# Later pooled attention for one batch, sums of squares on other engines, and a one-pass summation in a fused attention and two-layer kernel

## The chip, the cores and the metric

The kernel runs on one core of a Trainium2 chip. The metric is the device time of one execution in microseconds (us). The kernel before took 986.81, 987.01 and 991.75 us in three runs; the median is 987.01 us.

## The reference

Three parts follow one another, and each one's output is the next one's input. All matrices come in with 64-bit floating point weights, while `q`, `k`, `v` and `x` have 32 bits.

```
q, k, v: (4, 8, 576, 64)
out_d  = softmax(mean4(q) @ mean4(k).T / 8) @ mean4(v)    # pooled over groups of 4 positions
local  = softmax(masked(q @ k.T / 8, |i - j| < 4)) @ v     # 7 neighbours
x  = repeat4(out_d) + local                                # (2304, 512)
h  = x @ w_in                                              # (2304, 2048)
x  = (max(h, 0) + alpha * min(h, 0)) @ w_out               # (2304, 512), "layer one"
xn = x / sqrt(mean(x * x) + 1e-6) * rms_g
x  = (silu(xn @ w_gate) * (xn @ w_val)) @ w_o2             # d_ff 1536, "layer two"
```

## The kernel before, in words

**Numbers.** A large product runs in three passes of 16-bit matmuls: both factors are split into a high and a low 16-bit part (`split`: ScalarE writes the high part, VectorE the rest). Each factor is first scaled by a power of two that comes from a sum of its squares: of `v` for the attention's output (`scale_x`, from the tile `vm`), and of each weight piece (`s1`, `s2`). A weight piece is loaded as 64-bit numbers in two halves, decoded to 32 bits in a slot `wc` (`Piece.load`, `Piece.decode`), summed (`Piece.square`), scaled (`scale_in`, `scale_out`, `scale2`) and split. Layer one has twelve pieces, layer two has twelve more.

**Where the squares are summed.** For `v`, ScalarE squares half a head pair at a time and adds up along the row (L771 for batch 0 in `Dense.norm`, L606 for the others in `vnorm`). L771 uses the tile `T` as a place for the unwanted squares, and `T` is later filled with the transposed `q` and `k` (L787). For a weight piece, `square` has TensorE multiply the upper 16 bits of twelve 128-column blocks by themselves (L1121, into `sqps`), and VectorE reads the diagonal (L1122).

**Order of the program.** Batch 0 has its pooled and local attention as dense matmuls (`Dense`, three column blocks c = 0, 1, 2 of 192 positions). Stages `h0`, `h1`, `h2` compute `h` for these blocks (tile `hps`, L1336), `o0` and `o1` the second product of layer one (tile `acc`, L1349); stage `c3` does both for the first block of batch 1. Then come `m2` (layer two: `gps` L1428, `oacc` L1457) and `m1` (layer one) in turn, each for 384 positions. A matmul stage hands a share of the list `feed[stage]` out between its steps: weight pieces (`prep_out`, `prep2_tasks`), pooled attention of batches 1 to 3 (`down_tasks`), and local attention of 192 positions (`local_tasks`, groups 4 to 11).

**Local attention.** A group makes six products of `q` with `k` windows (896 elements each; VectorE L480 and GpSimd in turn), sums each over 64 with L491, takes the softmax, and makes six products with `v` (L528). A product `prod` lies as 2 positions x 7 neighbours x 64. The sum over the 7 neighbours is three adds on VectorE in place (L541, 384, 256 and 128 elements).

**What sets the order on an engine.** `issue_order` takes every instruction with its buffer and data dependencies, gives it a cost by a formula, and runs a list scheduler 20 times; the best order is fixed for each engine. An engine works through its list in that order, so an instruction that waits holds up all behind it.

**Slots.** The buffers `u0` to `u12` hold first the pieces of `w_in`, later other tiles, and at last layer two's weights: piece number k of layer two is decoded into one slot and its split parts go into the slot that piece k - 1 was decoded into (`RING`).

## Time and profile before

| | us |
|---|---|
| median of three runs | 987.01 |
| the profiled execution, its own time | 985.53 |
| its span, first to last instruction | 983.8 |
| TensorE (PE) busy | 934.7 |
| VectorE (DVE) busy | 680.0 |
| ScalarE (ACT) busy | 469.5 |
| GpSimd (POOL) busy | 139.3 |
| granted TensorE clock, mean | 0.987 of 2.4 GHz |

The profiled execution took 1.7 us more than its span: that much lies around the first and the last instruction. PE's busy time counts a matmul until its result has landed, so matmuls overlap in it, and a busy PE isn't PE at its peak. In the page's forty slices PE is at 3, 7, 7, 8, 8 and 8 tenths in the first six, and then at 9 or more.

### The profile page before, as it was taken

The page shows a single profiled execution, that of the slowest core. Times are in us where ns is not written, and L with a number is a line of the kernel's source. Part 1 is how long each engine was busy: PE and PEld are TensorE (multiplying, and loading weights), DVE is VectorE, ACT ScalarE, POOL GpSimd, SP SyncE. Part 2 cuts the span into 40 slices and gives each one's busy share as a digit, 9 for nine tenths or more (in the row PEclk, how much of TensorE's full clock was granted, in tenths as well). Part 3 has the DMA queues.
Part 4 walks back from the last instruction along what each step waited for, and adds up shares of the span by engine and source line. Part 5 has one row for each costly group of instructions (what it writes and reads, how often), then busy time and mean ns, then how long its engine had stood idle before and what let it go on. Part 6 is the DMA issues. An engine that isn't in the chain of part 4 may idle for free.

```text
span 983.8 us, 16822 instructions
## 1 busy us (share of the span) xinstructions
PE 934.7 (95%) x6562; PEld 605.3 (62%) x6562; DVE 680.0 (69%) x1461; ACT 469.5 (48%) x1099; POOL 139.3 (14%) x120
## 2 busy tenths in 40 slices
PE   3778889999999999999999999999999999999998
PEld 2567677689865555556666665555556666555554
DVE  2689878989999979999676899972343352442333
ACT  4779999867554661233485242221232432321322
POOL 4511011211211022332001222210000000000000
PEclk9987999999999999999999999999999999999999
DMA  9847555566120331221221111110000000000000
GB/s 229 239 121 218 150 169 161 194 208 194 53 89 13 102 122 60 81 65 37 61 97 33 49 37 47 32 32 1 11 22 2 1 1 1 1 1 5 29 1 32
DMA packets 54205, 73.81 MB, mean 75 GB/s; under 512 B 22682, under 2 KB 35630, under 8 KB 54126
## 3 DMA queue, kind: packets, MB, share of 16 engines
q1 hardware_dynamic: 54126, 72.74, 24.9%
q8 instruction: 51, 0.84, 0.3%
q14 instruction: 28, 0.23, 0.1%
HBM read 68.01 MB, written 4.72 MB: 74 GB/s over the span
## 4 chain that ended last, share of the span: by engine, by line
PE 72%; ACT 11%; DVE 8%; DMA 6%; issue 2%; SPq 1%; ACTq 0%; DVEq 0%
PE gps L1428 25%; PE acc L1349 16%; PE hps L1336 13%; PE oacc L1457 12%; DMA out_dram<-ob 3%; DMA sdv<-in_v_dram 2%; ACT dls L896 2%; ACT wr L1103 1%; DVE prod L541 1%; DVE w L376 1%; ACT wr L1106 1%; ACT wi L375 1%; ACT g L1340 1%; PE lsps L876 1%; PE avps L684 1%
## 5 line engine op out<-in xcount | busy, mean ns | idle before, releaser
L1336 PE MATMUL hps<-xt,wi 128*128 128x192 f16 (+1 forms) x1536 | 339.1, 290 | 7.4 <-DVE g L376 5.7
L1428 PE MATMUL gps<-x,w 128*128 128x384 f16 x1728 | 342.2, 326 | 0.8 <-DVE th L1439 0.4
L1349 PE MATMUL acc<-ghl,wo 128*128 128x384 f16 (+1 forms) x960 | 256.1, 310 | 2.4 <-ACT ghl L375 1.8
L1428 PEld LDWEIGHTS <-w 128*128 128x128 f16 x1728 | 169.0, 98 | 113.5 <-issue 1.9
L1457 PE MATMUL oacc<-w,uhl 128*128 128x512 f16 x630 | 190.6, 379 | 1.6 <-ACT ob L1513 1.6
L1336 PEld LDWEIGHTS <-wi 128*128 128x128 f16 x1536 | 148.1, 100 | 58.5 <-issue 8.6
L1349 PEld LDWEIGHTS <-wo 128*128 128x128 f16 x1344 | 129.7, 99 | 65.1 <-issue 4.9
L1342 DVE SCALAR_TENSOR_TENSOR hps<-g,oma,hps 128x192 f32<-128x192 f32 (+1 forms) x128 | 65.8, 516 | 68.8 <-ACT g L1340 68.1
L1437 ACT ACTIVATE th<-gps,tsc 128x384 f32<-128x384 f32 x72 | 41.7, 579 | 131.0 <-PE gps L1428 130.6
L1457 PEld LDWEIGHTS <-uhl 128*128 128x128 f16 x630 | 61.6, 98 | 66.3 <-issue 2.4
L1439 DVE SCALAR_TENSOR_TENSOR th<-th,gps 128x384 f32<-128x384 f32 x72 | 39.7, 551 | 90.5 <-ACT th L1437 89.8
L1448 ACT ACTIVATE uhl<-gps 128x384 f16<-128x384 f32 x72 | 41.7, 579 | 108.3 <-DVE gps L1442 97.9
L1340 ACT ACTIVATE g<-hps 128x384 f32<-128x384 f32 x96 | 47.3, 493 | 95.3 <-PE hps L1336 95.1
L480 POOL TENSOR_TENSOR prod<-cq,ckv 128x896 f32<-128x896 f32 x24 | 55.5, 2313 | 218.6 <-DVE ls L491 68.4
L528 POOL TENSOR_TENSOR prod<-ls,ckv 128x896 f32<-128x896 f32 x24 | 45.2, 1884 | 151.0 <-DVE lo L541 58.9
L1449 DVE TENSOR_TENSOR uhl<-gps,uhl 128x384 f16<-128x384 f32 x72 | 45.3, 630 | 27.8 <-ACT uhl L1448 27.4
L375 ACT ACTIVATE ghl<-hps,sc 128x384 f16<-128x384 f32 x72 | 41.8, 580 | 44.9 <-DVE hps L1342 44.0
L376 DVE SCALAR_TENSOR_TENSOR ghl<-hps,sc,ghl 128x384 f16<-128x384 f32 x72 | 44.2, 613 | 22.8 <-ACT ghl L375 22.4
L1349 PE MATMUL acc<-g,wo 128*128 128x384 f16 (+1 forms) x384 | 59.1, 286 | 0.0
L541 DVE TENSOR_TENSOR prod<-prod 128x384 f32<-128x384 f32 (+1 forms) x96 | 50.1, 535 | 2.9 <-POOL prod L528 2.9
L1103 ACT ACTIVATE wr<-wr 128x768 f32<-128x768 f32 (+1 forms) x48 | 42.3, 882 | 20.4 <-DMA wr<-in_moe_w_in_dram 10.4
L491 DVE TENSOR_REDUCE ls<-prod 128x14 f32<-128x896 f32 x48 | 51.1, 1075 | 0.0
(233 smaller groups left out, 1172.5 us busy)
## 6 DMA issues: line engine op xcount, KB each, us to landing
wr<-in_moe_w_out_dram SPq DMA_DIRECT2D x18, 512.0 KB
wr<-in_moe_w_in_dram SPq DMA_DIRECT2D x10, 768.0 KB
wr<-in_moe_w_gate_dram SPq DMA_DIRECT2D x8, 768.0 KB
wr<-in_moe_w_val_dram SPq DMA_DIRECT2D x8, 768.0 KB
ckv<-in_k_dram SPq DMA_DIRECT2D x7, 768.0 KB
ckv<-in_v_dram SPq DMA_DIRECT2D x7, 768.0 KB
wr<-in_moe_w_out_dram SPq DMA_DIRECT2D x20, 256.0 KB
out_dram<-ob SPq DMA_DIRECT2D x13, 256.0 KB
```

The source lines that it names most:

```text
L375: nc.scalar.activation(out=hi, in_=src, func=AF.Copy, scale=s)
L376: nc.vector.scalar_tensor_tensor(out=lo, in0=src, scalar=s, in1=hi, op0=ALU.mult, op1=ALU.subtract)
L480: engs[i].tensor_tensor(out=pr, in0=view(st["q"][:, j, t:t + TP], [[D, TP], [0, ND], [1, D]]), in1=view(st["k"][:, j, t:t + TP], [[D, TP], ...
L491: nc.vector.tensor_reduce(out=st["s"][:, j, t:t + TP], in_=st.pop(("p", i)), axis=AX.X, op=ALU.add)
L541: add = lambda o, a, c: nc.vector.tensor_tensor(out=o, in0=a, in1=c, op=ALU.add)
L1103: nc.scalar.activation(out=hi.bitcast(F32), in_=hi.bitcast(F32), func=AF.Prelu, scale=2.0 ** -112, alpha=2.0 ** 32)
L1336: nc.tensor.matmul(ps[:, j], wi[:, f + j, a, kk * 128:(kk + 1) * 128], x[:, b_, kk, c0:c0 + n], start=(i == 0), stop=(i == 3 * KK - 1))
L1340: nc.scalar.activation(out=g, in_=ps, func=AF.Relu, scale=-1.0)
L1342: nc.vector.scalar_tensor_tensor(out=ps[:, j], in0=g[:, j], scalar=oma[:, f + j:f + j + 1], in1=ps[:, j], op0=ALU.mult, op1=ALU.add)
L1349: nc.tensor.matmul(acc[e], wo_f(f)[:, a, e * 128:(e + 1) * 128], hl[:, b_], start=(f == 0 and i == 0), stop=(f == NF - 1 and i == 2))
L1428: nc.tensor.matmul(ps, w2_t[i0 + f // 3].rearrange("p a (k c) -> p a k c", k=KK)[:, a, kk, (f % 3) * 128:(f % 3 + 1) * 128], xh[:, b_, kk] ...
L1457: nc.tensor.matmul(acc[tt], t[:, a, tt * 128:(tt + 1) * 128], w[:, b_, f % 3], start=(f in first and i == 0), stop=(f in last and i == 2))
```

## The change

Five things change.

1. The sums of squares of `v` for batches 0 and 1 go from ScalarE to TensorE and VectorE (`vsum`: eight matmuls of 128 columns for each of four head pairs, then one VectorE read of the diagonal).
2. The sums of squares of layer two's twelve pieces go from TensorE and VectorE to ScalarE: one pass over 1536 elements, with the unwanted squares written into the slot that will hold the piece's split parts (`w2_tile`).
3. Batch 1's pooled attention (`d1`) loads into the slots `u3`, `u4`, `u5` and not into a part of `wo`, and stands in `h1`'s list, where it stood before the first matmul stage.
4. The sum over the 7 neighbours is one VectorE reduction that reads every 64th element.
5. The lists of the later stages are dealt out otherwise (layer two's pieces begin in `o0`, one local group of `m2` 0 goes to `m2` 1, one of `m2` 1 to `m1` 2); the scheduler has 40 rounds; four small VectorE steps of `pow2` and `scale2` are merged.

```
-def issue_order(tc, nc, groups, rounds=20):
+def issue_order(tc, nc, groups, rounds=40):
...
+    def vsum(b, h, x):
+        if h == 0:
+            vm_t[b] = att.tile([128, HP], F32, tag="vm", name="vm")
+        ps = ps_t.tile([128, 128], F32, tag="at", name="vqps")
+        up = x.bitcast(BF)[:, 1::2]
+        for i in range(8):
+            nc.tensor.matmul(ps, up[:, i * 128:(i + 1) * 128], up[:, i * 128:(i + 1) * 128], start=(i == 0), stop=(i == 7))
+        nc.vector.scalar_tensor_tensor(out=ps, in0=ps, scalar=1.0, in1=ident, op0=ALU.mult, op1=ALU.mult,
+                                       accum_out=vm_t[b][:, h:h + 1])
...
         def vnorm():
+            if solo_v:
+                st["buf"] = prod_p.tile([SH, 4 * SD + 4 * D], F32, tag="prod", name="dd")
+                vsum(b, h, st["v"].rearrange("p a j r -> p (a j r)"))
+                return
...
-            for a in range(2):
-                nc.scalar.activation(out=self.st[h]["T"][0:SH, 0, W:W + 8 * D], in_=vt[:, a * 8 * D:(a + 1) * 8 * D], func=AF.Square,
-                                     accum_out=vm_t[b][0:SH, 2 * h + a:2 * h + a + 1])
+            vsum(self.b, h, self.st[h]["v"])
...
         def square(self, acc):
+            if self.w is not w_in and self.w is not w_out:
+                nc.scalar.activation(out=self.junk[:, 0:UW], in_=self.c[:, 0:UW], func=AF.Square, accum_out=acc)
+                return
...
-    def local(g, mul="GVGVGV", av=True, tags=(None, None, None), **kw):
+    def local(g, mul="GVGVGV", av=False, tags=(None, None, None), **kw):
...
-    d1 = down(1, 5, tags=tuple(wd[:, i * 1024:(i + 1) * 1024] for i in range(3)))
+    d1 = down(1, 5, tags=("u3", "u4", "u5"))
     run_all(d0)
     run_all(pi)
...
-    run_all(d1)
...
-        "h1": weave(c2, po[1]),
-        "h2": weave(c3, po[2] + pr2[0]),
-        "o0": pr2[1][:20],
-        "c3": pr2[1][20:]+pr2[2],
-        ("m2", 0): weave(pr2[3], local(4) + local(5)),
-        ("m2", 1): down(2) + local(6) + local(7),
-        ("m1", 2): local(8),
+        "h1": weave(c2, po[1]) + d1,
+        "h2": weave(po[2],c3),
+        "o0": pr2[0]+pr2[1],
+        "o1": [],
+        "c3": pr2[2],
+        ("m2", 0): weave(pr2[3],local(4)),
+        ("m2", 1): local(5)+down(2)+local(6),
+        ("m1", 2): local(7)+local(8),
```

With `av=False` the sum over the neighbours is the branch of `red_av` that stood there unused:

```
nc.vector.tensor_reduce(out=st["o"][:, t:t + TP, j], in_=pr.rearrange("p t n d -> p t d n"), axis=AX.X, op=ALU.add)
```

**How the order moves.** First ScalarE's list just ahead of the first step of `h0` (`g<-hps`, the first read of a finished `hps`). In these names `dd` with `dsum` and `dd<-dd` are batch 1's pooled softmax, `wi` the split of `w_in`, `wr` the decoding of a weight half. Before:

```order
L634 ACTIVATE qkT<-qkps 128x144
L375 ACTIVATE xt<-dxs,sc 128x192
L375 ACTIVATE wi<-wc,swi 128x512
L375 ACTIVATE xt<-dxs,sc 128x192
L375 ACTIVATE wi<-wc,swi 128x512
L896 ACTIVATE dls,dlsum<-lsps,dlm 96x102 x2
L653 ACTIVATE dd,dsum<-sps,dm 72x144 x4
L896 ACTIVATE dls,dlsum<-lsps,dlm 96x102 x4
L663 ACTIVATE dd<-dd,dsum 72x144 x4
L1340 ACTIVATE g<-hps 128x384
```

and in the change:

```order
L373 ACTIVATE wi<-wc,swi 128x512 x3
L1109 ACTIVATE wr<-wr 128x768
L373 ACTIVATE wi<-wc,swi 128x512
L1112 ACTIVATE wr<-wr,nhalf 128x768
L373 ACTIVATE wi<-wc,swi 128x512 x2
L1109 ACTIVATE wr<-wr 128x256
L1109 ACTIVATE wr<-wr 128x768
L1109 ACTIVATE wr<-wr 128x256
L1112 ACTIVATE wr<-wr,nhalf 128x768
L1356 ACTIVATE g<-hps 128x384
```

Batch 1's softmax steps have left this place, and the decoding of `w_out` has come in.

Second, layer two's squares. Before, on TensorE in stage `c3`, the blocks of a piece (`sqps<-wc`) stand between the matmuls of layer one:

```order
L1121 LDWEIGHTS wc
L1121 MATMUL sqps<-wc 128x128
L1336 LDWEIGHTS wi
L1336 MATMUL hps<-xt,wi 128x192
L1349 LDWEIGHTS wo
L1349 MATMUL acc_3053<-ghl,wo 128x192
L1336 LDWEIGHTS wi
L1336 MATMUL hps<-xt,wi 128x192
L1121 LDWEIGHTS wc
L1121 MATMUL sqps<-wc 128x128
```

In the change they are gone there, and ScalarE's list in the same stage has a square (`w_3487,s_114<-wc`) between the split of the piece ahead (`w_3353<-wc`) and its own (`w_3487<-wc`):

```order
L1356 ACTIVATE g<-hps 128x384
L1112 ACTIVATE wr<-wr,nhalf 128x768
L373 ACTIVATE w_3353<-wc,sw_117 128x1536
L373 ACTIVATE ghl<-hps,sc 128x2x192
L1356 ACTIVATE g<-hps 128x384
L1123 ACTIVATE w_3487,s_114<-wc 128x1536
L373 ACTIVATE ghl<-hps,sc 128x2x192
L1109 ACTIVATE wr<-wr 128x768
L373 ACTIVATE w_3487<-wc,sw_117 128x1536
```

So a square now stands in line with the steps `g` and `ghl` that the matmuls of `c3` need.

Third, VectorE's list in a layer-two stage, `m2` 2. `th`, `gps` and `uhl` are the steps that the matmuls wait for. Before, with the three adds:

```order
L1439 SCALAR_TENSOR_TENSOR th<-th,gps 128x384
L541 TENSOR_TENSOR prod<-prod 128x2x192
L1442 SCALAR_TENSOR_TENSOR gps<-th,kap,gps 128x384
L528 TENSOR_TENSOR prod<-ls,ckv 128x896
L1449 TENSOR_TENSOR uhl<-gps,uhl 128x384
L541 TENSOR_TENSOR prod<-prod 128x2x2x64
L541 TENSOR_TENSOR prod<-prod 128x2x192
L541 TENSOR_TENSOR lo<-prod 128x2x64
L541 TENSOR_TENSOR prod<-prod 128x2x2x64
L1310 TENSOR_TENSOR ra<-x_7086,rps 128x384
L541 TENSOR_TENSOR lo<-prod 128x2x64
```

and in the change, with the one reduction `lo<-prod`:

```order
L1455 SCALAR_TENSOR_TENSOR th<-th,gps 128x384
L526 TENSOR_TENSOR prod<-ls,ckv 128x896
L1458 SCALAR_TENSOR_TENSOR gps<-th,kap,gps 128x384
L544 TENSOR_REDUCE lo<-prod 128x2x64
L1465 TENSOR_TENSOR uhl<-gps,uhl 128x384
L1326 TENSOR_TENSOR ra<-x_6914,rps 128x384
L544 TENSOR_REDUCE lo<-prod 128x2x64
L1326 TENSOR_TENSOR ra<-x_6914,rps 128x384
L526 TENSOR_TENSOR prod<-ls,ckv 128x896
L544 TENSOR_REDUCE lo<-prod 128x2x64
```

Two short adds fewer stand between the steps that TensorE needs, and each sum is one instruction.

## Rows read from the trace of the kernel before

**Rows 1.** The page's busy time of each engine, share of the span, instructions.
```profile
PE 934.7 (95%) x6562; PEld 605.3 (62%) x6562; DVE 680.0 (69%) x1461; ACT 469.5 (48%) x1099; POOL 139.3 (14%) x120
```

**Rows 2.** Busy time in stretches: us, PE, PEld, DVE, ACT, POOL, PEclk, DMA, GB/s.
```profile
57.00:84.00 27.00, 20.43 (x195) 17.51 (x191) 25.25 (x75) 22.54 (x89) 2.13 (x2) 0.75 0.45 129
84.00:124.00 40.00, 33.54 (x330) 27.11 (x329) 34.93 (x79) 39.92 (x108) 2.40 (x6) 0.87 0.65 187
124.00:166.00 42.00, 39.18 (x467) 34.05 (x468) 32.50 (x94) 40.12 (x120) 5.51 (x6) 1.00 0.59 175
166.00:226.00 60.00, 59.58 (x542) 46.17 (x540) 54.50 (x109) 43.46 (x77) 15.22 (x8) 1.00 0.57 191
226.00:265.00 39.00, 38.95 (x475) 37.93 (x473) 37.22 (x87) 28.77 (x42) 6.49 (x3) 1.00 0.39 123
265.00:353.00 88.00, 86.82 (x603) 53.99 (x603) 82.77 (x207) 50.84 (x117) 8.25 (x4) 1.00 0.24 73
...
427.00:496.00 69.00, 67.13 (x419) 40.68 (x417) 59.82 (x114) 28.18 (x67) 12.99 (x6) 1.00 0.20 58
...
569.00:642.00 73.00, 73.00 (x425) 42.08 (x424) 68.17 (x141) 21.50 (x42) 19.50 (x12) 1.00 0.12 31
```

**Rows 3.** Groups by line and shape: the squares of weight pieces on PE.
```profile
L1121 PE MATMUL sqps<-wc 128*128 128x128 bf16 x212 | 34.7, 232 | 2.9 <-DVE sqps L1122 2.1 <-DVE wc L1108 0.4 <-ACT outd L853 0.3
```

**Rows 4.** PE's instructions in order of time, in stage c3: start, duration.
```profile
238.01 0.22 PE L1121 MATMUL sqps<-wc 128*128 128x128 bf16 x1
238.07 0.24 PE L1336 MATMUL hps<-xt,wi 128*128 128x192 f16 x1
238.15 0.22 PE L1121 MATMUL sqps<-wc 128*128 128x128 bf16 x1
238.21 0.24 PE L1349 MATMUL acc<-ghl,wo 128*128 128x192 f16 x1
```

**Rows 5.** ACT's instructions in order of time: squares of v, first transposes.
```profile
14.30 0.63 ACT L771 ACTIVATE T<-sdv 72x512 f32<-72x512 f32 x1 [0.33 <-DMA sdv<-in_v_dram]
...
15.06 0.63 ACT L771 ACTIVATE T<-sdv 72x512 f32<-72x512 f32 x1
...
15.81 1.20 ACT L787 ACTIVATE T<-tps 128x288 f32<-128x288 f32 x2
...
62.29 0.66 ACT L606 ACTIVATE dd<-wo 72x512 f32<-72x512 f32 x1
...
63.07 0.63 ACT L606 ACTIVATE dd<-wo 72x512 f32<-72x512 f32 x1
```

**Rows 6.** The chain of waits between 80 and 84 us: start, length, what.
```profile
80.22 1.43 ACT dd L653 x8
...
82.94 1.22 ACT dd L663 x4
```

**Rows 7.** Groups by line and shape: ACT's pass over a piece of layer two.
```profile
L375 ACT ACTIVATE w<-wc,sw 128x1536 f16<-128x1536 f32 x12 | 18.9, 1574 | 6.1 <-DVE sw L366 6.1
```

**Rows 8.** Groups by line and shape, DVE: reduction of neighbouring elements; the three adds.
```profile
L491 DVE TENSOR_REDUCE ls<-prod 128x14 f32<-128x896 f32 x48 | 51.1, 1075 | 0.0
...
L541 DVE TENSOR_TENSOR prod<-prod 128x384 f32<-128x384 f32 x48 | 27.4, 573 | 2.9 <-POOL prod L528 2.9
...
L541 DVE TENSOR_TENSOR lo<-prod 128x128 f32<-128x128 f32 x48 | 25.1, 524 | 0.1
...
L541 DVE TENSOR_TENSOR prod<-prod 128x256 f32<-128x256 f32 x48 | 23.7, 496 | 0.0
```

**Rows 9.** Groups by line and shape: spread writes (L787), L674 without; L575 spread reads.
```profile
L787 ACT ACTIVATE T<-tps 128x288 f32<-128x288 f32 x16 | 10.0, 707 | 2.2 <-PE tps L786 2.0
...
L674 ACT ACTIVATE aT<-atps 72x288 f32<-72x288 f32 x24 | 9.3, 413 | 3.7 <-PE atps L672 3.7
...
L575 DVE TENSOR_TENSOR xs<-xps,outd 128x192 f32<-128x192 f32 x16 | 7.8, 488 | 0.7 <-PE xps L562 0.7
...
L575 DVE TENSOR_TENSOR xs<-xps,outd 128x64 f32<-128x64 f32 x16 | 4.0, 252 | 2.8 <-PE xps L562 2.8
```

More of the change, by code (lines that the diff above doesn't have):

```diff
@@ L360, in pow2 @@
     def pow2(x, e, s, p, src=None):
-        if src is not None:
-            nc.vector.tensor_scalar(out=x, in0=src, scalar1=LEAST, scalar2=None, op0=ALU.max)
         xb, eb_, sb = (t.bitcast(I32) for t in (x, e, s))
-        nc.vector.tensor_scalar(out=xb, in0=xb, scalar1=1, scalar2=0x7F800000, op0=ALU.logical_shift_right,
+        nc.vector.tensor_scalar(out=xb, in0=xb if src is None else src.bitcast(I32), scalar1=1, scalar2=0x7F800000, op0=ALU.logical_shift_right,
                                 op1=ALU.bitwise_and)
@@ L764, in norm @@
         def norm(self, h):
-            b = self.b
-            if h == 0:
-                vm_t[b] = att.tile([128, 2 * HP], F32, tag="vm", name="vm")
-                nc.vector.memset(vm_t[b], 0.0)
-            vt = self.st[h]["v"]
-            for a in range(2):
-                nc.scalar.activation(out=self.st[h]["T"][0:SH, 0, W:W + 8 * D], in_=vt[:, a * 8 * D:(a + 1) * 8 * D], func=AF.Square,
-                                     accum_out=vm_t[b][0:SH, 2 * h + a:2 * h + a + 1])
+            vsum(self.b, h, self.st[h]["v"])
             if h == HP - 1:
-                scale_x(b)
+                scale_x(self.b)
         def tr(self, h):
@@ L1139, with prep @@
     p2 = [w2_piece(i) for i in range(12)]
-    def prep(p, acc):
+    def prep(p, acc, junk=None):
         def ld(h):
@@ L1148, in sq @@
         def sq():
+            if junk is not None:
+                p.junk = junk()
             p.square(acc)
@@ L1218, in f @@
             y = s2[:, i:i + 1]
-            nc.vector.tensor_scalar(out=y, in0=over_parts(y), scalar1=LEAST, scalar2=None, op0=ALU.max)
             e, sc_ = eb2[:, i:i + 1], sw2[:, i:i + 1]
-            pow2(y, e, sc_, P_W)
+            pow2(y, e, sc_, P_W, over_parts(y))
             if i < 4:
@@ L1233, in scale2_all, with w2_tile, f @@
         nc.vector.tensor_reduce(out=col(INV2), in_=inv2, axis=AX.X, op=ALU.max)
+        nc.vector.tensor_scalar(out=col(INV2), in0=col(INV2), scalar1=LEAST * LEAST, scalar2=None, op0=ALU.max)
         nc.vector.reciprocal(col(TS), col(INV2))
         nc.vector.tensor_scalar(out=kap, in0=inv2, scalar1=col(TS), scalar2=2.0 ** -P_U, op0=ALU.mult, op1=ALU.mult)
+    def w2_tile(i):
+        def f():
+            w2_t[i] = wts.tile([128, 2, UW], F16, tag=f"u{RING[W2_AT[i]]}", name="w2")
+            return w2_t[i][:, 0]
+        return f
     def split2(i):
@@ L1239, in f @@
             p = p2[i]
-            w = wts.tile([128, 2, UW], F16, tag=f"u{RING[W2_AT[i]]}", name="w2")
-            w2_t[i] = w
+            w = w2_t[i]
             split(w[:, 0], w[:, 1], p.c, sw2[:, i:i + 1])
@@ L1247, in prep2_tasks @@
         for i in W2_ORDER:
-            out.append(prep(p2[i], s2[:, i:i + 1]) + [scale2(i), split2(i)])
+            out.append(prep(p2[i], s2[:, i:i + 1], w2_tile(i)) + [scale2(i), split2(i)])
         out[-1].append(scale2_all)
```

1 line of the change is left out of this document (added).

## The prediction

> **What bounds the kernel now.** I read the page's busy line first: PE is busy for 934.7 of 983.8 us, the others for 680 us or less [rows 1]. An average over the run doesn't say where those 934.7 us lie, so I read the busy time in stretches next, cut at the first residual step of each stage [rows 2]. Two regimes are to be seen there. From 166 us on PE has no gaps worth naming (59.58 of 60, 38.95 of 39, 86.82 of 88, 67.13 of 69, 73.00 of 73), so an instruction taken from PE there is time won, and one added is time lost. Ahead of 166 us it is ScalarE: 39.92 of 40 us, then 40.12 of 42, while PE has gaps and VectorE is at 34.93 and 32.50. So the start is paid in ScalarE's work, up to the point where PE is full.
>
> The third thing to see is VectorE behind the full PE. It holds 82.77 of 88 us and 68.17 of 73 in the stretches that carry local attention, 94% and 93%. In those stages I take 94% as what it can hold while it still serves PE in time: the traced kernel shows nothing fuller in a long stretch. Last I read durations by line and shape, and the order of both kernels for what stands in line with what.
>
> **The squares of layer two leave PE: -8 us.** 144 matmuls go. Each holds its own 0.22 us in the records, but matmuls overlap: the next one starts 0.06 us behind a squares matmul and 0.08 us behind a 192-column one [rows 4], so a slot costs 0.060 us. The group shows 212 such matmuls with a mean of 232 ns [rows 3]; 212 by 232 ns is 49 us where its busy time says 34.7, which again says that the records overlap. One piece (12 matmuls) falls ahead of 166 us, where PE has gaps. The other 132 by 0.060 us give **-7.9 us** straight off the full PE. The 64 matmuls that come in for `v` stand ahead of 166 us and cost PE nothing as long as its gaps there (6.5 us of 40, 2.8 of 42 [rows 2]) hold 64 by 0.060 = 3.8 us.
>
> **The same squares on ScalarE: +2 us (0 to +17).** One pass over 1536 elements is not in the trace with a square; the nearest row is the split's high part of the same shape, 1.574 us [rows 7]. Twelve are 18.9 us of ScalarE. One falls ahead of 166 us; of the rest ten stand in 166 to 265 us and just behind it, where ScalarE is busy for 43.46 + 28.77 = 72.2 of 99 us [rows 2]; with 10 by 1.574 = 15.7 that is 88, 89%, still below the 95% that it held in 124 to 166. So most is covered. But a square stands in front of `g` and `ghl`, and PE waits for these; now and then one will come late by its 1.57 us. I take one to two of them. If that cover is gone (every one delays PE), it is 11 by 1.574 = 17 us.
>
> **The start: -8 us (0 to -14).** ScalarE loses 16 passes over `v`: eight of L771 and eight of L606, each 0.63 to 0.66 us, at a spacing of 0.76 and 0.78 us [rows 5]. By durations that is 10.2 us, by spacings 12.3; I take 11. ScalarE gains, in the same stretch, one layer-two square (1.6) and, by the order, five splits of `w_out` that come forward (512 elements, 0.63 each by the L771 row, 3.2). Net -6.2. The first evacuation of transposes (L787 at 15.81) stood behind L771's writes to the same tile (14.30 to 15.69) [rows 5]; about 1.5 us of that go too, together **-8 us** until PE is full. At the most I add the pooled softmax `dd` that leaves the chain at 80 to 84 us, 1.43 + 1.22 = 2.65 us [rows 6], and the 3.2 us of splits if they were idle filling: -14. `d1` isn't gone, though: its loads, softmax and products come later in `h1`, where ScalarE was as full (40.12 of 42), so I count its move at nothing. Its place behind `h0` also takes its DMAs from `wo`'s space to `u3` to `u5`; DMA engines are busy 0.59 to 0.65 of that time [rows 2]. At the least it's 0: VectorE gets the diagonal reads and `d1`'s steps there, some 5 us by the order, on 34.93 of 40 and 32.50 of 42, and could come last instead.
>
> **The strided sum: +13 us (0 to +24).** This is the largest term, and the trace doesn't show its price. Three adds, 573 + 524 + 496 ns = 1.593 us, become one reduction over 896 elements that hops by 64 elements at each step [rows 8]. Below, the bound is the reduction of the same 896 elements in their order: 1.075 us [rows 8]. Above, there are two rows for spread access [rows 9]. A VectorE step that reads spread elements takes 488 ns for 192 elements and 252 for 64: (488 - 252) / 128 = 1.84 ns an element and 134 ns fixed, so 896 x 1.84 + 134 = 1.78 us. ScalarE's spread write of 288 elements takes 707 where the plain one takes 413, (707 - 413) / 288 = 1.02 ns an element more; laid on the reduction it is 1.075 + 0.914 = 1.99 us. I take 1.78: it is the same engine, and a read. By that the edit makes each sum longer, by 0.19 us, not shorter.
>
> The page titled "Vector Engine (DVE) Microarchitecture Reference" of the Trainium skill (section 5.2, measured stream behaviour on trn2) says the same more sharply: a port keeps its rate only for runs of two or more adjacent words, and one that hops at every element takes 1.73 to 1.76 ns, in one case 2.50. An estimate by these is 1.63 to 2.3 us for this reduction; the trace's 1.84 ns an element lies between.
>
> What it does in a stage depends on the deal of local groups too. `m1` 2 has two groups' worth, 12 reductions where 9 sums stood. Its VectorE is 59.82 of 69 us; less 9 x 1.593 = 14.3, plus 12 x 1.78 = 21.4, plus five more L491 (5.4) and some 3 us of other steps of the group that comes in: 75 of 69 us. `m2` 2 by the order has 12 where 8 stood: 68.17 - 12.7 + 21.4 = 77 of 73 us. The excess over the whole stretch is 6 + 4 = 10 us, over 94% of it 10.5 + 8.3 = 19; neighbours can take some over, so **+13**. At 1.075 both are 67 to 69 us, and the term is about 0; at 1.99 the excess is 10 + 8 to 15 + 13 us, and I take 24.
>
> The merged scale steps, the 40 rounds and the rest of the new deal I cost at nothing: they lie on VectorE ahead of the splits, which are early in stages where PE is fed by pieces long since there.
>
> **Sum.** -8 - 8 + 2 + 13 = -1 us against the profiled execution of 985.5, thus 984.5. The median of the runs lies 1.5 us above that execution, so against it the forecast is **986 us**. A measurement of this kernel can tell 0.5% from no change, so "same" is 982.1 to 991.9 us.
>
> **The rivals.**
>
> - **The stride costs nothing** (a reduction takes 1.075 us whatever it reads). For it: the kernel's other reduction runs at 1.2 ns an element. Against: the spread rows [rows 9]. Then the last term is 0: 985.5 - 8 - 8 + 2 = 971.5, against the median **973**, faster.
> - **VectorE becomes the bound, slower than before.** If a reduction takes 1.99 us, the price of the second spread row, or more, `m1` 2 and `m2` 2 are over-full by the 24 us above: 985.5 - 14 + 24 = 995.5, against the median **997**. For it: the row [rows 9], and VectorE at 94% in these stages. Against: PE's other stages have slack on VectorE that could take groups over (59.82 of 69). The point from which it decides is where 24 reductions' growth outweighs 14 us, near 1.8 us each. The same page's 2.50 ns would put it well beyond: an estimate by that is 2.3 us each.
> - **The squares hold ScalarE's queue.** A square writes into the slot that the piece before was decoded into, so it waits until VectorE has split that piece; `g` and `ghl` of the matmul stage wait behind it. If each of 11 costs its 1.574 us on PE, the term is 17 and not 2: 984.5 + 15 = 999.5, against the median **1001**. Against: 89% of ScalarE, and PE in `c3` has the work of two products.
> - **The start gives nothing** (VectorE or the DMAs come last there): 984.5 + 8, against the median **994**.
>
> **How the numbers follow.** The forecast gets 0.35; its own range, with the start from 0 to -14 and the sum from 1.7 to 1.85 us, is 978 to 994. The stride that costs nothing gets 0.33, VectorE as the bound 0.20, the queue of squares 0.06, the empty start 0.06. The cases lie on both sides, so the range must hold most: from 967 (the first rival with a start of -14) to 1003 (the second with a start of -2). Faster by over 0.5%: all of the first rival but a little, and a quarter of the forecast's, 0.40. Within 0.5%: over half of the forecast's and some of the empty start, 0.25. Slower: the second and third rivals, half of the empty start and a fifth of the forecast's, 0.35.
>
> **What would show it.** The squares: no `sqps` from `gps`' weights, and PE in 166 to 265 us with fewer instructions and no new gaps. The start: PE full some 8 us earlier than 166 us, with ScalarE as busy as before up to there. The strided sum: the mean of `lo<-prod` as a reduction, about 1.78 us; 1.08 makes the first rival right, 2 or more the second. `m1` 2 and `m2` 2: VectorE at 97% or more and PE with gaps that end on `th` or `uhl`. ScalarE's squares: gaps of PE that end on `g` or `ghl` between 166 and 300 us, 1.6 us each, if the queue is the trouble. The forecast is wrong if the reduction is far from 1.78 us, or if it is near it and PE in those two stages has no gaps.

## The result and the profile after

The changed kernel takes **998.24 us** (median of 4 runs, 995.70 to 1000.68) against 986.91 us for the kernel before: a ratio of 1.0109, 95% interval 1.0072 to 1.0146. It is slower, by 1.1%. The forecast was 986 us, with -1 us for the change. The forecast's range (967 to 1003) holds the time, but the change went the other way, and two of its terms were wrong in their mechanism. The profiled execution took 1000.68 us with a span of 998.8.

The page's busy line of the changed kernel:

```profile
PE 939.8 (94%) x6482; PEld 604.1 (60%) x6482; DVE 690.6 (69%) x1337; ACT 475.3 (48%) x1091; POOL 132.1 (13%) x120
```

VectorE is busy 10.6 us more than before [rows 1], ScalarE 5.8 more. PE has 80 matmuls fewer (144 less 64). The stretches of the changed kernel, cut at the same stage steps (us, PE, PEld, DVE, ACT, POOL, PEclk, DMA, GB/s):

```profile
125.00:171.00 46.00, 43.24 (x478) 35.92 (x475) 37.94 (x106) 43.90 (x148) 5.06 (x6) 0.96 0.47 136
171.00:229.00 58.00, 57.75 (x515) 44.60 (x514) 52.98 (x77) 45.68 (x78) 14.40 (x8) 1.00 0.62 201
229.00:270.00 41.00, 36.91 (x418) 34.88 (x416) 36.77 (x76) 34.81 (x50) 0.00 (x0) 1.00 0.42 137
270.00:345.00 75.00, 75.00 (x459) 44.80 (x457) 68.03 (x132) 36.66 (x59) 11.99 (x6) 1.00 0.09 32
...
427.00:502.00 75.00, 70.09 (x432) 42.41 (x430) 73.23 (x113) 24.93 (x53) 20.81 (x11) 1.00 0.19 57
...
578.00:655.00 77.00, 73.17 (x419) 41.44 (x418) 75.13 (x127) 20.11 (x40) 23.11 (x14) 1.00 0.15 39
```

Against [rows 2] two places stand out. The start is over at 171 and not 166 us. And PE has gaps in the stages that it filled before: 36.91 of 41, 70.09 of 75 and 73.17 of 77 us, in the last two with VectorE at 73.23 and 75.13, 98%. The groups by line and shape of the changed kernel that answer to [rows 3, 7, 8]:

```profile
L544 DVE TENSOR_REDUCE lo<-prod 128x128 f32<-128x896 f32 x48 | 82.8, 1727 | 0.0
...
L489 DVE TENSOR_REDUCE ls<-prod 128x14 f32<-128x896 f32 x48 | 51.2, 1077 | 0.0
...
L1123 ACT ACTIVATE w<-wc 128x1536 f16<-128x1536 f32 x12 | 17.8, 1485 | 7.0 <-DVE w L374 3.9 <-DVE ry L1309 2.5 <-DVE ry L1306 0.6
...
L1130 PE MATMUL sqps<-wc 128*128 128x128 bf16 x68 | 10.1, 271 | 4.8 <-DVE wc L1118 3.6 <-DVE sqps L1131 1.1
```

The strided reduction takes 1.727 us, the contiguous one 1.077; the square on ScalarE 1.485; of the 212 squares of `wc` on TensorE 68 are left, those of layer one. Who PE waits for between 427 and 655 us (engine, line, releaser: us, times, longest us):

```profile
PE xps L560 <- DVE lo L544: 2.8, 3, 1.3
PE hps L1352 <- DVE ghl L374: 2.5, 4, 0.9
PE gps L1444 <- DVE th L1455: 2.4, 2, 1.4
PE acc L1365 <- ACT ghl L373: 1.2, 1, 1.2
PE xps L560 <- DVE inv L1377: 1.1, 1, 1.1
```

7.7 of these 10.0 us end on VectorE's `lo`, `ghl` and `th`: the strided sums themselves and the steps that stand behind them.

To tell early from late I count from each profiled trace how much of PE's main work (the columns of `hps`, `acc`, `gps`, `oacc`, at 0.163 us per 384 columns, 798.0 us in all) has been started by 225 us, and call "lost late" what the rest of the span has beyond the rest of that work: (span - 225) - (798.0 - done). What is lost late thus holds PE's small matmuls and transposes too; the least in any kernel here is 44.1 us. A number in these two columns is worked out, not printed by a view, and comes from one execution, which can lie some us from the median (e4's took 1007.44 us, e7's 989.24); small differences in them are weak. "Time" is the median of the runs, the ratio that to runs of the kernel before on the same chip; it is not the quotient of the medians.

```
kernel                                    time    ratio (95%)               span   done 225  lost late
before                                   986.91                             983.8     90.3     51.1
changed                                  998.24  1.0109 (1.0072 - 1.0146)   998.8     87.7     63.5
e1  changed, adds                        981.17  0.9925 (0.9899 - 0.9952)   979.7     90.5     47.2
e2  changed, d1 at its old place         992.31  1.0056 (1.0036 - 1.0076)   990.7     92.2     59.9
e3  before, strided                     1008.15  1.0202 (1.0174 - 1.0231)  1001.7     93.9     72.6
e4  changed, w2 squares on PE           1001.59  1.0149 (1.0118 - 1.0180)  1005.4     88.1     70.5
e5  e1, v squares on ACT                 982.25  0.9962 (0.9941 - 0.9984)   980.2     90.0     47.2
e6  e1, d1 at its old place              981.38  0.9943 (0.9922 - 0.9963)   980.7     87.9     45.6
e7  e1, w2 squares on PE                 984.21  1.0001 (0.9975 - 1.0027)   987.5     89.2     53.7
e8  neighbours innermost                 982.21  0.9951 (0.9929 - 0.9972)   979.4     91.4     47.8
e9  e8 on GpSimd's, adds on the others   989.12  1.0033 (1.0009 - 1.0058)   992.2     82.8     52.0
e10 e1, diagonal reads five times        987.44  1.0015 (0.9988 - 1.0042)   986.8     80.3     44.1
e11 e1, old deal                         986.08  1.0011 (0.9986 - 1.0035)   983.7     92.0     52.7
e12 half the sums strided                998.39  1.0124 (1.0086 - 1.0163)   997.4     86.5     60.9
e13 changed, right price                 985.15  0.9985 (0.9969 - 1.0001)   983.8     88.8     49.6
e14 e1, extra ScalarE                   1000.20  1.0148 (1.0120 - 1.0175)  1002.8     71.1     50.9
e15 e1, extra VectorE                    985.89  0.9993 (0.9975 - 1.0011)   984.3     85.3     46.6
e16 e8, right price                      976.39  0.9906 (0.9879 - 0.9934)   974.9     92.4     44.3
e17 e12, right price                     992.45  1.0074 (1.0048 - 1.0100)   990.3     86.0     53.3
e18 e1, 3 rounds                         981.77  0.9964 (0.9939 - 0.9988)   981.4     86.9     45.3
```

So the change lost 2.6 us by 225 us and 12.4 after it, 15.0 in the spans.

### The profile page after: what moved, and what is told of

It is laid out like the page before. It is cut to its first block, busy times and chain, and to the rows that moved or that the text cites. A ratio compares the mean times of both kernels' runs of the same rounds, so it can differ in the third digit from the quotient of the medians.

```text
span 998.8 us, 16517 instructions
## 1 busy us (share of the span) xinstructions
PE 939.8 (94%) x6482; PEld 604.1 (60%) x6482; DVE 690.6 (69%) x1337; ACT 475.3 (48%) x1091; POOL 132.1 (13%) x120
## 4 chain that ended last, share of the span: by engine, by line
PE 58%; DVE 19%; ACT 10%; DMA 8%; issue 4%; SPq 1%; ACTq 0%; DVEq 0%
PE gps L1444 21%; PE hps L1352 12%; PE acc L1365 10%; PE oacc L1473 10%; DVE lo L544 7%; DMA out_dram<-ob 2%; DVE prod L526 2%; ACT wr L1112 1%; DMA sdv<-in_v_dram 1%; ACT dls L902 1%; ACT wr L1109 1%; DVE hps L1358 1%; DMA wr<-in_moe_w_gate_dram 1%; DVE gps L1458 1%; DVE wc L1114 1%
## 5 line engine op out<-in xcount | busy, mean ns | idle before, releaser
L1365 PE MATMUL acc<-ghl,wo 128*128 128x384 f16 (+1 forms) x960 | 247.8, 310 | 1.6 <-ACT ghl L373 1.2
L1444 PEld LDWEIGHTS <-w 128*128 128x128 f16 x1728 | 169.7, 99 | 122.3 <-issue 10.2
L1473 PE MATMUL oacc<-w,uhl 128*128 128x512 f16 x630 | 193.2, 379 | 2.5 <-ACT ob L1529 1.5
L544 DVE TENSOR_REDUCE lo<-prod 128x128 f32<-128x896 f32 x48 | 82.8, 1727 | 0.0
L478 POOL TENSOR_TENSOR prod<-cq,ckv 128x896 f32<-128x896 f32 x24 | 51.8, 2156 | 234.5 <-PE avps L697 54.2
L526 POOL TENSOR_TENSOR prod<-ls,ckv 128x896 f32<-128x896 f32 x24 | 41.5, 1727 | 145.8 <-DVE lo L544 66.6
```

The source lines that it names most:

```text
L478: engs[i].tensor_tensor(out=pr, in0=view(st["q"][:, j, t:t + TP], [[D, TP], [0, ND], [1, D]]), in1=view(st["k"][:, j, t:t + TP], [[D, TP], ...
L526: engs[i].tensor_tensor(out=pr, in0=view(st["s"][:, j, t:t + TP], [[ND, TP], [1, ND], [0, D]]), in1=view(st["v"][:, j, t:t + TP], [[D, TP] ...
L544: nc.vector.tensor_reduce(out=st["o"][:, t:t + TP, j], in_=pr.rearrange("p t n d -> p t d n"), axis=AX.X, op=ALU.add)
L1365: nc.tensor.matmul(acc[e], wo_f(f)[:, a, e * 128:(e + 1) * 128], hl[:, b_], start=(f == 0 and i == 0), stop=(f == NF - 1 and i == 2))
L1444: nc.tensor.matmul(ps, w2_t[i0 + f // 3].rearrange("p a (k c) -> p a k c", k=KK)[:, a, kk, (f % 3) * 128:(f % 3 + 1) * 128], xh[:, b_, kk] ...
L1473: nc.tensor.matmul(acc[tt], t[:, a, tt * 128:(tt + 1) * 128], w[:, b_, f % 3], start=(f in first and i == 0), stop=(f in last and i == 2))
```

## Experiments: the strided sum

**e1, the adds back.**

```
-    def local(g, mul="GVGVGV", av=False, ...
+    def local(g, mul="GVGVGV", av=True, ...
```

> The changed kernel with the three adds back; all else as changed. Theory S (the strided reduction, 1.727 us against some 1.39 to 1.59 for the adds, fills VectorE in the stages from the second layer-two stage to the fourth and costs the 15 us that the changed kernel's stage marks lose between 427 and 724 us): 998.2 - 15 = 983 us, 980 to 987, with VectorE at 95% or less in these stages. Rival D (the new deal of the local groups, two in one stage, costs it, whatever the sum is made of): 993 to 998 us, the loss still between 427 and 724 us.

981.17 us, ratio 0.9925: better than both kernels. Late loss falls from 63.5 to 47.2. The strided sum costs 16.3 us late, and the rest of the change is worth some 4 to 7 us (4.1 by the spans, 7.4 by the ratio). Rival D falls.

**e3, the stride alone.** The kernel before with `av=False`.

> The kernel before with the strided reduction in place of the three adds, nothing else. Theory S: each of 48 sums grows by 0.13 (1.727 - 1.593) to 0.34 us; where VectorE was at 93 to 94% the growth shows: 987 + 5 to 12, 992 to 999 us. Rival D (only the new deal overfills VectorE): 986 to 989 us, since the old deal had at most 8 to 9 sums a stage.

1008.15 us: more than either theory gave. The late loss grows by 21.5 us with the old deal's 8 or 9 sums in a stage. VectorE's time doesn't explain all of it: 48 sums of 1.719 us in place of 1.593 are 6 us, and the whole busy time rose by 697.9 - 680.0 = 17.9. How much of it is order (see e13) is not shown: this kernel was not run with another order.

**e8, no strided read.** The product is written so that the reduction reads neighbouring elements.

```
-            pr = prod_p.tile([128, TP, ND, D], ...)
+            pr = prod_p.tile([128, TP, D, ND], ...)
...
-                out=pr,
+                out=pr.rearrange("p t d n -> p t n d"),
...
-  tensor_reduce(..., in_=pr.rearrange("p t n d -> p t d n"), ...)
+  tensor_reduce(..., in_=pr, ...)
```

> The changed kernel, but each product of p and v is written with the 7 neighbours innermost, so that the reduction reads neighbouring elements and the product writes every 7th. If the stride is what costs 0.65 us a reduction: the reduction takes 1.08 us, as L489's does. The price may go to the product: 1.08 us to 1.7 on VectorE; GpSimd's half is off the path. Then 24 VectorE products cost 0 to 15 us, 48 reductions give 31: 998.2 - 17 or more, 970 to 985 us. If a reduction with 128 results costs 1.7 us whatever it reads: reduction 1.7 us, 998 us or more.

982.21 us, inside the expectation. Its groups (L526 is the product, L544 the sum):

```profile
L544 DVE TENSOR_REDUCE lo<-prod 128x128 f32<-128x896 f32 x48 | 51.4, 1073 | 0.0
...
L526 POOL TENSOR_TENSOR prod<-ls,ckv 128x896 f32<-128x896 f32 x24 | 44.9, 1873 | 135.8 <-DVE lo L544 60.0 <-DVE ls L520 38.4 <-issue 31.7
L526 DVE TENSOR_TENSOR prod<-ls,ckv 128x896 f32<-128x896 f32 x24 | 43.7, 1822 | 0.0
```

The reduction falls from 1.727 to 1.073 us, and VectorE's product, which now writes every 7th element, goes from 1.119 to 1.822. So the stride has its price on whichever side it is, read or write; on GpSimd the spread write takes 1.873, where the plain product took 1.884 in the kernel before and 1.727 in the changed one. VectorE does 673.8 us in all.

**e12, half of the sums strided** (those whose product GpSimd makes).

```
-            if av_pool:
+            if i % 2:
```

> The changed kernel with 24 of the 48 sums strided (those whose product GpSimd does not make, or the other half, in turn) and 24 by adds. If each strided sum costs TensorE its 0.35 us, whatever else VectorE does: half the loss, 989 to 991 us. If there is a limit of VectorE below which the stride is free: 24 x 0.25 = 6 us of VectorE are within its room, and the time is 981 to 984 us.

998.39 us: as much as with all. Both expectations missed, so the loss is neither proportional to the number of strided sums nor a plain limit on VectorE's time. Its groups show a second cost:

```profile
L544 DVE TENSOR_REDUCE lo<-prod 128x128 f32<-128x896 f32 x24 | 41.1, 1714 | 0.0
...
L526 DVE TENSOR_TENSOR prod<-ls,ckv 128x896 f32<-128x896 f32 x24 | 39.5, 1644 | 0.0
```

VectorE's products L526 take 1.644 us on the mean instead of 1.119. By the starts and ends of the records, the eleven that began while a GpSimd product was running took 1.41 to 2.72 us, the other 13 took 1.07 to 1.09 (more in the last section). None of the 24 strided reductions ran beside a GpSimd product here.

**e9, each way where it is cheaper.** The layout of e8 for GpSimd's products, plain products and adds for VectorE's (`if engs[i] is not nc.gpsimd`).

> The changed kernel with each of the two ways where it is cheaper: products made on GpSimd are written with the neighbours innermost (GpSimd took 1.87 us for that, 1.73 for the plain ones) and reduced in 1.07 us; products made on VectorE stay plain and are summed by the three adds. VectorE does 24 x 0.5 = 12 us less than with the adds alone. If VectorE still holds TensorE up with the adds: 972 to 978 us. If with the adds the later stages are TensorE's and VectorE's time there is worth nothing: 980 to 982 us, as with the adds alone.

989.12 us: both missed. VectorE's busy time is 691.2 us where the reckoning made it 668: the 15 of its products that met one of GpSimd's took 1.94 us on the mean. And 7.7 us are gone by 225 us, nearly all of it ahead of the local attention that the edit changes. Another order of one and the same program moved that by 3.6 us (e18 below); the rest is not explained.

**e13, the planner told.** This came of e3 and e12. `issue_order` prices a VectorE instruction by

```
            return 89 + n / (1.92 if fast else 0.96) + 60 * (extra > 0)
```

with n its elements: 89 + 896 / 0.96 = 1022 ns for a sum, strided or not, and 489 + 356 + 222 = 1067 for the three adds. Whoever reads that expects a small gain. The edit:

```
+            if n == 896 and any(list(a.ap)[-1][0] > 1 for a in (o, ins[0])):
+                return 89 + 1.83 * n
             return 89 + n / (1.92 if fast else 0.96) + 60 * (extra > 0)
```

> The changed kernel, strided sums as changed, but the planner's formula prices such a reduction at 1.73 us and not at 1.02. If the order made for a wrong price is what costs (steps that TensorE needs put behind sums that end 0.7 us later than planned): most of the 17 us comes back, 983 to 988 us. If it is VectorE's time: 995 to 1000 us as before.

**985.15 us**, 13 us less than the changed kernel, with the same instructions: 48 strided sums of 1.723 us. Of the 16.3 us of late loss 13.9 go (63.5 to 49.6). VectorE's time is not what came back: it is busy for 700.1 us here, 9.5 more than in the changed kernel. The difference is in the order. From 427 to 655 us PE's waits add up to 4.5 us, where the changed kernel has 10.0 and the kernel before 3.0. VectorE's instructions in order of time in the same stage, first the changed kernel (start, duration, no idle time between):

```profile
443.36 1.08 DVE L526 TENSOR_TENSOR prod<-ls,ckv 128x896 f32<-128x896 f32 x1
444.37 1.71 DVE L544 TENSOR_REDUCE lo<-prod 128x128 f32<-128x896 f32 x1
445.99 0.62 DVE L374 SCALAR_TENSOR_TENSOR ghl<-hps,sc,ghl 128x384 f16<-128x384 f32 x1
446.51 1.76 DVE L544 TENSOR_REDUCE lo<-prod 128x128 f32<-128x896 f32 x1
448.16 0.64 DVE L1358 SCALAR_TENSOR_TENSOR hps<-g,oma,hps 128x384 f32<-128x384 f32 x1
448.68 1.11 DVE L526 TENSOR_TENSOR prod<-ls,ckv 128x896 f32<-128x896 f32 x1
449.69 1.72 DVE L544 TENSOR_REDUCE lo<-prod 128x128 f32<-128x896 f32 x1
451.30 0.64 DVE L374 SCALAR_TENSOR_TENSOR ghl<-hps,sc,ghl 128x384 f16<-128x384 f32 x1
```

Then with the right price:

```profile
443.53 0.61 DVE L1360 SCALAR_TENSOR_TENSOR hps<-g,oma,hps 128x384 f32<-128x384 f32 x1
444.05 1.74 DVE L546 TENSOR_REDUCE lo<-prod 128x128 f32<-128x896 f32 x1
445.71 0.60 DVE L376 SCALAR_TENSOR_TENSOR ghl<-hps,sc,ghl 128x384 f16<-128x384 f32 x1
446.23 1.07 DVE L528 TENSOR_TENSOR prod<-ls,ckv 128x896 f32<-128x896 f32 x1
447.23 0.61 DVE L1360 SCALAR_TENSOR_TENSOR hps<-g,oma,hps 128x384 f32<-128x384 f32 x1
447.76 1.71 DVE L546 TENSOR_REDUCE lo<-prod 128x128 f32<-128x896 f32 x1
449.38 0.60 DVE L376 SCALAR_TENSOR_TENSOR ghl<-hps,sc,ghl 128x384 f16<-128x384 f32 x1
```

In the changed kernel a product and a sum stand in a row, with no step that PE needs (`hps` or `ghl`) between them. By the formula the two take 2 x 1.02 = 2.04 us, on the chip 1.73 + 1.08 = 2.8. In the lines with the right price such a step stands on either side of each sum: `hps` and `ghl` get their turn every 1.5 to 2.2 us (443.53, 445.71, 447.23, 449.38) and not every 2.2 to 3.1 (445.99, 448.16, 451.30). In the four densest batches of six sums of the changed kernel the first and the last start 12.4 to 12.9 us apart, in the same four batches of e13 13.3 to 17.7. What that does to PE, busy time of 443 to 459 us by engine, in the changed kernel:

```profile
443.00:459.00 16.00, 14.29 (x88) 8.59 (x87) 16.00 (x17) 3.68 (x7) 5.62 (x4) 1.00 0.14 46
```

and in e13:

```profile
443.00:459.00 16.00, 16.00 (x102) 9.93 (x100) 16.00 (x20) 4.29 (x8) 5.86 (x3) 1.00 0.16 50
```

VectorE is full in both; PE runs 88 matmuls in the one and 102 in the other. A full VectorE costs PE little as long as what PE needs comes first.

Could it be one lucky order? The late column speaks against it: the five kernels with strided reads at the old price (changed, e2, e3, e4, e12) lose 59.9 to 72.6 us late, and every other kernel, in whatever order, 44.1 to 53.7. e17 and e16, the other two with the new price, come next.

**e17, half strided, told.** e12 with e13's edit.

> The kernel with 24 strided sums and 24 by adds, and the planner told 1.73 us for a strided one. If the wrong price was what cost in the untold one (998.4 us): 983 to 987 us, between the adds alone (981) and all strided with the right price (985). If VectorE's 24 slower products beside GpSimd are what cost there: 994 us or more.

992.45 us: 6 us of the 17 come back, neither expectation's number. The order was part of it. What is left (late loss 53.3, done by 225 us 86.0) is not told apart here from the slower two-source steps beside GpSimd (VectorE's products still took 1.40 us on the mean) and the order's luck.

**e16, neighbours innermost, told.** e8 with e13's edit.

> The kernel whose products are written with the neighbours innermost, the planner told 1.73 us for a VectorE product that writes every 7th element (it was priced at 1.02 and took 1.82; 24 of them). If a wrong price costs where VectorE is short: below the 982.2 us of the untold one, 976 to 980 us. If the room that the cheap reduction (1.07 us) leaves has hidden the wrong price: 980 to 983 us.

**976.39 us**, ratio 0.9906 (0.9879 to 0.9934): the best of all, faster than the kernel before by 0.9% and than the changed one by 2.2%. Against e8 the price alone gave 5.8 us. The page's busy line of it shows VectorE 3 us below the kernel before and PE at 929.9:

```profile
PE 929.9 (95%) x6482; PEld 598.9 (61%) x6482; DVE 677.0 (69%) x1337; ACT 475.7 (49%) x1091; POOL 136.1 (14%) x120
```

## Experiments: squares, deal and start

**e4 and e7, layer two's squares back on TensorE** (`square` without its early return), in the changed kernel and in e1.

> The changed kernel with layer two's squares back on TensorE. If their leaving gave the 8 us less some 2 that was reckoned: 998.2 + 6 = 1004 us, 1002 to 1007. Rival (ScalarE's queue took the gain back, or VectorE's stages would have given the time anyway): 996 to 1000 us.

> The changed kernel with the adds back, and layer two's squares on TensorE as before. If 132 matmuls of 0.060 us are paid in full where TensorE is full, less 2 for ScalarE: 981 + 6 = 987 us. If the 3.4 us seen with the strided sum is all there is: 984.5 us. If ScalarE's queue takes it back: 981 us.

By medians 3.4 and 3.0 us, by the traces' late loss 7.0 and 6.5; but the profiled executions of these two took 5 to 6 us more than their medians, so the larger numbers are the weaker ones. The ratios' intervals overlap for e4 and don't for e7. So the squares' move is worth 3 to 7 us, half of the forecast's 6 or all of it. Of PE's waits from 166 to 300 us in the changed kernel, 4.8 us, 0.5 end on a square and none on ScalarE's `g` or `ghl`. The gap that is new from 229 to 270 us ends mostly on VectorE's `ry` (2.1 us, once).

**e11, the old deal** of the lists from `h2` to `m1` 2, in e1.

> The changed kernel with the adds back and the old deal of the lists from h2 to the third stage of layer one. If the new deal is worth something by itself: 984 to 988 us. If it only spreads VectorE's work, which has room with the adds: 980 to 983 us.

986.08 us, 4.9 more than e1, and 5.5 us more lost late, as the first expectation has it: with plain sums the new deal is worth that. I had reckoned nothing for it. The single prices don't simply add up: by medians the squares (3.0) and the deal (4.9) make 7.9 us, and e1 gains 5.7 on the kernel before.

**e2 and e6, batch 1's pooled attention at its old place**, in the changed kernel and in e1.

```
-    d1 = down(1, 5, tags=("u3", "u4", "u5"))
+    d1 = down(1, 5, tags=tuple(wd[:, i * 1024:(i + 1) * 1024] for i in range(3)))
...
+    run_all(d1)
...
-        "h1": weave(c2, po[1]) + d1,
+        "h1": weave(c2, po[1]),
```

> The changed kernel with batch 1's pooled attention back in its old place, ahead of the first matmul stage, and its old buffers. Theory P (its place in h1 is what turned the expected 8 us of the start into a loss of 5): the first product of layer one's second half starts 5 to 8 us earlier than 170.9 us, and the time is 990 to 993 us. Rival V (the start is lost to VectorE's diagonal reads and the decoding of w_out, which stay): within 2 us of 998.2. Rival C (the old place puts the softmax back on the chain ahead of the first g): h0 4 us later, the start the same or worse, 998 to 1001 us.

> The changed kernel with both suspects undone: the three adds, and batch 1's pooled attention ahead of the first matmul stage in its old buffers. If the two losses are separate (17 and 6 us in the runs with one of them undone): 998.2 - 17 - 6 = 975 us, 973 to 978, first product of the second half at 160 to 163 us. If the start is lost only while VectorE is short of time later: the same as with the adds alone, 981 us.

992.31 and 981.38 us. The first is the time that theory P named, but its 6 us are not there in the second, so theory P falls: the place is worth nothing once the sums are plain. Both find another order throughout; e2 gains 4.5 us by 225 and 3.6 later, e6 loses 2.6 and gains 1.6.

**e5, the squares of `v` back on ScalarE**, in e1 (`Dense.norm` and `vnorm` as before).

> The changed kernel with the adds back, and the squares of v on ScalarE as before. If moving them off ScalarE gave the 6 to 8 us that the forecast reckoned: 981 + 7 = 988 us, first product of the second half at 174 to 176 us. If VectorE and the loads end the start, not ScalarE: 979 to 983 us.

982.25 us, as the second expectation has it; 90.0 us of PE's work by 225 us, where e1 has 90.5. Moving 16 passes off ScalarE gave some 1 us, next to nothing.

**e10, the diagonal of `v`'s squares read five times**, in e1.

> The changed kernel with the adds back, and each VectorE read of the diagonal of v's squares done five times (the result is the same): 32 more reads of 0.29 + 0.14 us, 13.8 us of VectorE ahead of 170 us. If VectorE ends the start: TensorE's progress at 170 us is 4 to 8 us less than with the adds alone and the time 985 to 990 us. If it is as indifferent as ScalarE was to 13.7 us of squares: 980 to 983 us.

987.44 us, 10.2 us less work by 225, as the first expectation has it. At first sight VectorE ends the start. But the reads stand in the chain from `v` to its scale, and the planner orders all anew. The next two hold the order still.

**e14 and e15, extra work at a fixed order**, in e1. 64 small steps on one engine, left out of what the planner orders; every other instruction keeps its place.

```
+        for _ in range(16 if b == 1 else 0):
+            nc.scalar.activation(out=idle, in_=ident, func=AF.Copy, scale=vm_t[b][:, h:h + 1])
```

> The changed kernel with the adds back and 64 extra ScalarE copies of 128 elements (about 0.2 us each, 13 to 18 us) strewn over h1 and h2; the order of all other work on every engine is exactly that of the run with the adds alone. If ScalarE ends the start, as the forecast took it: its TensorE work at 225 us falls by 10 us or more and the time is 991 to 999 us. If not: less than 4 us.

> The same with 64 extra VectorE steps of 128 elements (about 0.2 us each) in place of the ScalarE copies. If VectorE ends the start: 8 us or more, 989 to 995 us. If both engines' extras cost about their length, the start is a chain that runs through both; if neither, it is TensorE or the loads, and the time is 981 to 984 us for both.

The extra steps in the groups by line and shape, of e14:

```profile
L602 ACT ACTIVATE idle<-ident,vm 128x128 f32<-128x128 f32 x64 | 26.0, 407 | 2.2 <-DVE vqps L599 1.4
```

and of e15:

```profile
L602 DVE TENSOR_SCALAR idle<-ident,vm 128x128 f32<-128x128 f32 x64 | 19.3, 301 | 0.7
```

They took longer than expected, and the times are 1000.20 and 985.89 us. 26.0 us on ScalarE cost 19.4 us of PE's work by 225 us (71.1 against 90.5), 19.3 us on VectorE cost 5.2. But the copies are not evenly strewn: 26 of ScalarE's 64 stand in one row from 164.38 to 175.6 us. Busy time by engine from 102 to 164 and from 164 to 176 us (us, PE, PEld, DVE, ACT, POOL, PEclk, DMA, GB/s), in e14:

```profile
102.00:164.00 62.00, 53.75 (x556) 44.72 (x554) 43.46 (x120) 59.62 (x194) 5.33 (x10) 0.89 0.41 116
164.00:176.00 12.00, 1.54 (x17) 1.18 (x15) 0.31 (x5) 10.80 (x27) 0.00 (x0) 0.68 0.29 90
```

and in e1:

```profile
102.00:164.00 62.00, 56.38 (x643) 46.98 (x638) 52.34 (x143) 56.75 (x186) 6.97 (x12) 0.97 0.49 144
164.00:176.00 12.00, 12.00 (x120) 9.27 (x117) 9.24 (x26) 11.32 (x33) 2.18 (x3) 1.00 0.46 135
```

By 164 us the first 38 copies, 15.6 us, had cost PE's main work 3.1 us (34.2 against 37.3); behind the row of 26 it was 10.2 us short at 176 and 22.9 at 200. The granted clock was lower in both stretches too (0.89 against 0.97, 0.68 against 1.00), so a part may be the clock's. So PE depends on ScalarE in the start, and much more than on VectorE. But a us of ScalarE's work is not a us of PE's: what it costs depends on where it stands, and the run gives no price for work taken off elsewhere.

**e18, another order of the same program** (e1, `rounds=3`).

> The changed kernel with the adds back and the order search stopped after 3 rounds (10, 20 and 40 rounds give one and the same order). The program is the same; only the order differs. If the order's luck moves a kernel as much as the start's term: 4 to 10 us off 981, with TensorE's work at 225 us off by as much. If not: within 3 us.

981.77 us: the same time, as the second expectation has it. But 3.6 us less work by 225, and 1.9 less lost late. The luck of the order moves the start by almost half of the term that I had for it.

## Why the prediction was wrong, step by step

The sum was -1 us, the spans show +15.0. Of these 16 us the start is 10.6 (-8 against +2.6), the strided sum 3.3 (13 against 16.3), and all else 2.1 (-8 + 2 = -6 against 47.2 - 51.1 = -3.9).

**"The start: -8 us (0 to -14)" failed**; it was +2.6 by 225 us (87.7 against 90.3). That PE depends on ScalarE there was right (e14); that "the start is paid in ScalarE's work", us for us, was not. What was wrong is which of that work lay on the path. The forecast counted all 16 passes, but read the windows from 57 us on. Busy time by engine ahead of that and behind it, in the kernel before:

```profile
0.00:57.00 57.00, 35.46 (x226) 26.40 (x228) 27.58 (x80) 35.64 (x102) 25.84 (x54) 1.00 0.87 221
57.00:170.00 113.00, 97.07 (x1024) 81.30 (x1021) 96.38 (x258) 106.59 (x327) 11.70 (x16) 0.89 0.58 169
```

ScalarE's instructions in order of time, the fifth and the eighth of its L771 passes:

```profile
28.52 0.63 ACT L771 ACTIVATE T<-sdv 72x512 f32<-72x512 f32 x1 [0.65 <-DMA sdv<-in_v_dram]
...
36.04 0.63 ACT L771 ACTIVATE T<-sdv 72x512 f32<-72x512 f32 x1
```

and the two windows in the changed kernel:

```profile
0.00:57.00 57.00, 41.25 (x268) 30.46 (x268) 29.09 (x85) 31.14 (x96) 26.86 (x54) 1.00 0.80 204
57.00:170.00 113.00, 97.37 (x1003) 81.05 (x1004) 97.36 (x258) 102.89 (x293) 9.15 (x14) 0.89 0.55 171
```

All eight L771 passes lie between 14 and 37 us, where ScalarE had 21 of 57 us free. By the spacing that is 6.1 of the 12.3 us, and the wait of the first evacuation lies there too. In the changed kernel ScalarE has 4.5 us less to do there and 3.7 less behind it, and PE isn't further: of its main work 37.9 us have been started by 170 us, 40.7 in the kernel before. The other eight passes are 6.2 us, less the 1.6 and 3.2 that come forward: a gain of 1.4 us, not 8. That little is left agrees with e5, where all 16 passes back on ScalarE cost 0.5 us of work by 225 us. The 4 us between a gain of 1.4 and a loss of 2.6 are not settled: e18 shows 3.6 us for order alone.

**"The strided sum: +13 us" had the duration right and the mechanism wrong.** 1.78 us was reckoned from [rows 9], 1.727 measured; the row's step reads a TensorE result and also writes every second element, so that they agree so well is in part luck. By the page titled "Vector Engine (DVE) Microarchitecture Reference" of the Trainium skill, section 5.2, with its 1.73 to 1.76 ns for a port that hops at every element, the prediction's estimate began at 1.63 us; this case's 1.727 us for 896 elements, and e8's 1.822 us for a spread write, lie 6 and 12% above that. VectorE's load came as reckoned too: 73.23 and 75.13 us in `m1` 2 and `m2` 2, for 75 and 77. All the signs that the prediction named for this term were there (the duration, VectorE at 98%, gaps of PE that end on `th`), but they could not tell a lack of VectorE's time from a bad order of its steps. The cost late was 16.3 us (e1). But "94% as what it can hold while it still serves PE in time" is refuted by e13: this is what it holds with the right price, busy time from 427 to 496 and from 569 to 642 us of e13:

```profile
427.00:496.00 69.00, 66.33 (x411) 39.98 (x410) 68.36 (x105) 25.83 (x59) 16.39 (x9) 1.00 0.19 59
...
569.00:642.00 73.00, 72.30 (x421) 41.53 (x418) 69.77 (x118) 18.92 (x36) 20.18 (x12) 1.00 0.16 41
```

99% of the first stretch with PE at 66.33 of 69 us, 96% of the second with PE at 72.30 of 73. 13.9 of the 16.3 us were an order made for sums of 1.02 us. The planner's costs set the order, and the forecast did not ask what they say of the new instruction. Nor did it see what the adds' mean is made of: clear of GpSimd's products they took 0.547 + 0.413 + 0.279 = 1.24 us (by overlap of the records of before), 0.49 less than the strided sum. The rest of the 1.593 is time beside GpSimd's products, and another order moves it (1.565 in e1, so there a sum grew by 0.16, near the forecast's 0.19).

**"The squares of layer two leave PE" and "on ScalarE", -8 + 2: right in sign, and in size between half and all** (e4 and e7: 3 to 7 us). The rival of ScalarE's queue didn't come.

**The deal "at nothing" beside the sums failed**: e11 gives 5.5 us late to the new deal with plain sums. The merged scale steps were not tested by themselves; of the rounds, 3 do as well as 40 (e18).

**Of the rivals**, "VectorE becomes the bound" named 997 us, and 998 came, but not by its condition: it asked for 1.99 us a sum, and its point of decision was VectorE's time. That it came within 1 us is luck. "The start gives nothing" was nearest on the start and had a chance of 0.06; that VectorE or the DMAs come last there, as it said, is not shown. What happened adds up as a start of +2.6, strided sums in a bad order of +16.3, and a gain of the rest: 2.6 + 16.3 - (51.1 - 47.2) = 15.0 us.

## What to carry to other kernels

Where a planner fixes each engine's order from a cost formula, look up what the formula says of every instruction that an edit brings in, and compare with the trace: a price that is 0.7 us too low on 48 instructions cost 13 to 14 us here, and two lines in the formula gave them back. Before work taken from a bounding engine is counted as won, look at each instance's place in the timeline: half of it lay where that engine was idle for 21 of 57 us. A summation over strided elements paid for the stride once here, on the read or on the write. With the write spread, VectorE paid on 24 products instead of 48 sums, since GpSimd makes the other 24, in 1.87 us, where plain ones took 1.73 to 1.88; check both ways with the right price (976.4 us here).
